# Shifted score powers and scaled V rows on GpSimd in a gated mix of attention and a Mish layer

## The chip, the cores and the metric

The kernel runs on one core of a Trainium2 chip. The metric is the device time of one execution in microseconds (us); lower is better. The engines are TensorE (PE in the profile, with PEld for its weight loads), VectorE (DVE), ScalarE (ACT), GpSimd (POOL) and SyncE (SP), which issues the DMAs.

## The reference

All inputs are bf16. `x` is 1 x 2048 x 640; there are 32 heads of width 20, and the hidden layer has 1536 columns.

```python
g = sigmoid((x * gate_w).sum(-1, keepdims=True))
q, k, v = split_heads(x @ wqkv)                      # 32 heads, Dh = 20
a = (softmax(q @ k.T * Dh ** -0.5) @ v).merge() @ wo
h = x @ w1 + b1
b = (h * tanh(softplus(h))) @ w2                     # Mish
out = g * a + (1 - g) * b
```

## The kernel before

Heads are taken four at a time (a quad, index `p`, eight of them), and queries 512 at a time (`qc`, four of them). A pair (p, qc) is a group `G`; there are 32. For each group and each block `j` of 128 keys, PE computes four score tiles, one per head: keys on partitions, 512 queries in one bank of PSUM (line 1127). Then comes exp, then the product with V (PV, line 1220), which sums over `j` in the last PSUM bank. V lies in `VA` with a column of ones, so that the sum of the exps comes out with the product; `normalise` divides by it.

The exps are made in two ways. Most go through ACT, two or three banks at an instruction (line 1177, into the ring `E`). The others, called sets in this text (one `j` of one group, all four heads), go through DVE. Line 437 turns a score tile into a power of two by writing a scaled and offset number as int16 and reading the bits as bf16, one instruction per head into a tile `T` of 128 x 2048. Two more tiles are made from `T` by adding a constant to each 16-bit word (line 495, `SHIFT` 43 and 86). The three tiles go into PV in turn, the shifted ones against copies of V scaled by 0.793 and 0.629 (`VD`, line 388). So the saw teeth of three approximations are averaged, and one set has three PVs of four matmuls in place of one. `VD` holds the last `ND` blocks of keys of a quad, and has three buffers for the eight quads. A shift may be placed only once its quad's `VD` is there.

PE also runs the dense products in pieces (chains: q and k, V, the hidden layer `h`, `w2`, `wo`), where four matmuls of 32 columns of the array stand side by side (`product`, line 531). ACT runs Mish twice, over half of the hidden layer each time (line 814), with a change of its function table before and after.

The whole order is made when the kernel is built, by a planner written into the kernel. It keeps a clock for PE, ACT and DVE, gives each instruction a fixed cost by its kind, and at each tick lets each free engine choose its next work by rules (`step_pe`, `step_act`, `step_dve`). The rules have some twenty parameters, changed as the groups advance by the table `PLAN`. The result is a fixed program: each engine runs its instructions in that order and waits on semaphores. PE does not pass over an instruction whose input is late.

In the tail of the kernel `b` (already multiplied by 1 - g and stored in DRAM, line 854) is loaded again a row block at a time (`load_b`, line 893) and added to the product with `wo` (line 933). `load_b` is called when a row's `wo` chain begins, for that row and the next one. All these DMAs stand in SP's queue in the order in which the planner calls them, with the stores of `o_dram` and the transposing loads of `od`.

```python
for eng in ("DVE", "ACT", "PE"):
    if free[eng] <= t:
        cost = steps[eng](t)
```

Of the kernel before, what the change touches and what calls it, by code (L numbers as in the profile page):

```python
# [11 lines left out]
ALU = mybir.AluOpType  # L12
F32 = mybir.dt.float32
BF16 = mybir.dt.bfloat16
I16 = mybir.dt.int16
F16 = mybir.dt.float16
PSUM = bass.MemoryType.PSUM
DEBUG = False


class Chain:
# [34 lines left out]
EXP_S2S = {3: 1331.0, 2: 904.0, 1: 520.0}  # L56
EXP_DUR = {3: 1460.0, 2: 1035.0, 1: 630.0}
DVE_TAIL = 100.0
INF = 1.0e18


@with_exitstack
def kernel(
# [33 lines left out]
    RATIO = (1.0, 0.79296875, 0.62890625)  # L97
    BETA = -210.4127
    LOG2E = 1.4426950408889634
    ND = 6  # L100
    NLAST = 3
    NSB = 2
    NFILL = 2
# [59 lines left out]
    rule.WAIT1 = 0.0  # L163
    rule.WAIT2 = 100000.0
    rule.WAITU = 100000.0
    PLAN = {
        0.0: {'AHEAD': 5000.0, 'BEHIND': 6000.0, 'D2': 0.5, 'DQ': 1, 'DQ3': 2, 'DQ4': 2, 'ETIGHT': 0, 'HEAT': 0.9, 'HROOM': 0.0, 'KEEP3': 3, 'LEAD': 6, 'LOW': 0.5, 'MARGIN': 60.0, 'MERGE': 0, 'NEAR': 9, 'NOPEN': 3, 'PVMAX': 4, 'Q3': 2, 'ROOM': 200.0, 'SWTH': 520.0, 'VF': 0, 'VMIN': 2, 'WAIT1': 2000.0, 'WAIT2': 6000.0, 'WAITU': 100000.0},
        1.0: {'DQ3': 1, 'HROOM': 100.0, 'LOW': 0.6, 'MARGIN': 0.0, 'SWTH': 600.0, 'WAIT2': 100000.0},
        2.0: {'DQ': 2, 'KEEP3': 1, 'MARGIN': 30.0},
        3.0: {'VMIN': 1},  # L170
        4.0: {'NOPEN': 4},
        5.0: {'AHEAD': 2000.0, 'DQ3': 0, 'MERGE': 1, 'Q3': 3},
        6.0: {'LOW': 0.44, 'MERGE': 0, 'NOPEN': 3, 'SWTH': 300.0, 'VF': 2, 'WAIT2': 30000.0},
        7.0: {'DQ4': 3, 'NEAR': 7},
        8.0: {'BEHIND': 2000.0, 'KEEP3': 2},
        9.0: {'D2': 1.0, 'HROOM': -200.0, 'NOPEN': 4, 'VF': 1, 'VMIN': 3},
        10.0: {'BEHIND': 6000.0, 'HEAT': 0.7, 'HROOM': 0.0, 'KEEP3': 3, 'LEAD': 5, 'LOW': 0.53, 'MARGIN': 100.0, 'PVMAX': 2, 'ROOM': 100.0, 'SWTH': 450.0, 'VMIN': 1},
        11.0: {'AHEAD': 3000.0, 'VF': 2},
        12.0: {'NEAR': 12},
        13.0: {'AHEAD': 5000.0, 'PVMAX': 3},  # L180
        14.0: {'AHEAD': 2000.0, 'BEHIND': 4000.0, 'DQ': 1},
        15.0: {'LOW': 0.47, 'NEAR': 9, 'WAITU': -200000.0},
        16.0: {'DQ': 2, 'DQ3': 3, 'PVMAX': 4, 'SWTH': 250.0, 'WAITU': 100000.0},
        17.0: {'BEHIND': 2000.0, 'HROOM': 100.0, 'SWTH': 600.0},
        18.0: {'KEEP3': 2, 'MARGIN': 0.0, 'PVMAX': 3},
        19.0: {'BEHIND': 3000.0, 'KEEP3': 3, 'MARGIN': 100.0, 'NEAR': 12},
        20.0: {'MARGIN': 60.0, 'Q3': 1, 'VF': 0},
        21.0: {'LOW': 0.38, 'NEAR': 9, 'WAITU': -200000.0},
        22.0: {'BEHIND': 2000.0, 'DQ': 1, 'DQ3': 0, 'LOW': 0.53, 'ROOM': 300.0},
        23.0: {'HEAT': 0.8, 'WAITU': 100000.0},  # L190
        24.0: {'BEHIND': 6000.0, 'DQ4': 0},
        25.0: {'DQ4': 1, 'PVMAX': 4, 'WAITU': -200000.0},
        26.0: {'NOPEN': 2, 'WAITU': 0.0},
        28.0: {'NOPEN': 4},
        29.0: {'HEAT': 0.7},
        30.0: {'HEAT': 0.8, 'NEAR': 99, 'PVMAX': 3, 'SWTH': 450.0},
    }

    x2d = A_x[0]
    out2d = out[0]  # L200
# [154 lines left out]
    dve_q = []  # L355
    act_q = deque()
    seq = [0]
    free = {"PE": 0.0, "ACT": 0.0, "DVE": 0.0}
    mode = [None]
    prog = [0.0]  # L360
    s_left = [64] * NG
    idle = {"PE": 0.0, "ACT": 0.0, "DVE": 0.0}

    def dve(t, ready, cost, fn, prio=1, done=None, can=None, born=INF):
        seq[0] += 1
        dve_q.append((prio, ready, seq[0], cost, fn, done, can, born))


    T_slots = [Slot(f"T{i}") for i in range(NHOLD)]
# [13 lines left out]
    def make_vd(p, t):  # L383
        VD[p] = work.tile([P, ND, NSH, 4 * (DH + 1)], BF16, tag=f"VD{p % NLAST}", name="VD")
        left = [NSH]

        def scale(i, t):
            nc.vector.tensor_scalar(
                out=VD[p][:, :, i, :],
                in0=VA[:, NS - ND : NS, 4 * p : 4 * p + 4, :].rearrange("p j h d -> p j (h d)"),  # L390
                scalar1=RATIO[i + 1], scalar2=None, op0=ALU.mult,
            )

        def done(t):
            left[0] -= 1
            if left[0] == 0:
                vd_ready[p] = t

        for i in range(NSH):
            dve(t, t, 200.0, (lambda t, i=i: scale(i, t)), prio=1, done=done)  # L400

    def backlog(t):

# [83 lines left out]
    def d_shifts(d, t):  # L487
        G, j = d["G"], d["j"]
        pv_items[G].append((t, j, (0, d["T"], d["slot"])))

        def shift(i, t):
            slot = t_slot(U_slots, t)
            slot.users = 4
            tile_ = work.tile([P, 4 * QC], BF16, tag=slot.tag, name="T")
            nc.vector.tensor_scalar(  # L495
                out=tile_[:, :].bitcast(I16), in0=d["T"][:, :].bitcast(I16),
                scalar1=float(SHIFT[i]), scalar2=None, op0=ALU.add,
            )
            d["T%d" % i] = (tile_, slot)
            d["slot"].users -= 1  # L500
            d["slot"].free_at = max(d["slot"].free_at, t + 700.0)

        def can(t):
            return (
                pv_G[0] >= G and vd_ready.get(groups[G][0], INF) <= t
                and t_slot(U_slots, t) is not None
            )

        for i in range(1, NSH + 1):
            dve(  # L510
                t, t, 600.0, (lambda t, i=i: shift(i, t)), prio=2, can=can,
                done=lambda t, i=i: pv_items[G].append((t, j, (i,) + d["T%d" % i])),
            )

# [306 lines left out]
    def b_chain(s, half, start, due):  # L821
# [19 lines left out]
        def evac():  # L841
            ps = box["ps"]

            def copy(t):
                if half == 0:
                    bt[s] = work.tile([P, D], BF16, tag=f"bt{s % 2}", name="bt")
                nc.vector.tensor_scalar(
                    out=bt[s][:, half * HALF : (half + 1) * HALF], in0=ps[:, :],
                    scalar1=g1_t[:, s : s + 1], scalar2=None, op0=ALU.mult,
                )  # L850

            def done(t):
                if half == 1:
                    nc.sync.dma_start(out=b_dram[s * P : (s + 1) * P, :], in_=bt[s][:, :])

            return [(420.0, copy)], done

# [27 lines left out]
    bl_slots = ["bl0", "bl1", "wkp"]  # L885
    bl_tag = {}

    def load_b(s):
        if s not in bl and s < NS and bl_slots and b_left[s // NU] == 0:
            bl_tag[s] = bl_slots.pop()  # L890
            pool_ = consts if bl_tag[s] == "wkp" else work
            bl[s] = pool_.tile([P, D], BF16, tag=bl_tag[s], name="bl")
            nc.sync.dma_start(out=bl[s][:, :], in_=b_dram[s * P : (s + 1) * P, :])
# [4 lines left out]
    def wo_chain(s, half, start, due):  # L898
# [6 lines left out]
        def piece(k, t):  # L905
            if k == 0:
                box["ps"] = bank_tile([P, HALF])
                begun.add(s)
                load_b(s)
                load_b(s + 1)  # L910
                assert s in bl
            r = min(P, rows - k * P)
            product(
                box["ps"][:, :],
                od[c][0:r, k, u * P : (u + 1) * P],
                wo_sb[0][0:r, k, cols],
                start=(k == 0),
                stop=(k == n - 1),
            )

        def evac():
# [16 lines left out]
            def done(t):  # L938
# [7 lines left out]

        return Chain(
            start, due, mm_pieces(n, piece, HALF / 2.4 + 3), evac,
            lambda t: o_ready.get(c, INF) <= t and (
                s in bl or (len(bl_slots) > 0 and b_left[c] == 0)  # L950
            ) and (s in begun if half else tail or ot_free.get(s % NOT, 0.0) <= t),
        )


# [466 lines left out]
    def enter(kind):  # L1421
        sw = switch(kind)
        mode[0], tiles[0] = kind, tiling(kind)
        return sw

    work_log = deque()
    heats = [0]

    def note(t, cost, weight):
        work_log.append((t, cost * weight))  # L1430
# [5 lines left out]

    def step_pe(t):
        units = s_ready(t)
        want = sum(ch.share(prog[0]) for ch in shares)
        d_take(t)  # L1440
        stuck_ = blocked(t)
        end = not peek(1)
# [74 lines left out]
        if units:  # L1517
# [20 lines left out]
                    break  # L1538
            enter("S")
            note(t, MM, 0.25 * len(used))  # L1540
            return cost
        until = max(slack, 0.0)
        if in_use(t) >= NOUT:
# [76 lines left out]
            done(t + cost + DVE_TAIL + SEM)  # L1620
        return cost

    steps = {"PE": step_pe, "ACT": step_act, "DVE": step_dve}
    t = 0.0
    stuck = 0
    vd_next = 0
    plan = sorted(PLAN)
    while pv_G[0] < NG or chains or chain[0] or dve_q or act_q:
# [3 lines left out]
        kq_loads(t)  # L1632
# [53 lines left out]
    for u, half, eng in ((2, 0, 0), (2, 1, 0), (3, 0, 0), (3, 1, 1)):  # L1686
# [4 lines left out]
            nc.vector.tensor_copy(out=dst, in_=src)  # L1691
        if half:
            nc.sync.dma_start(out=rows_[u], in_=ots_[u][:, :])
    if DEBUG:
        print("model end us", t / 1e3, "last exp", last_exp[0] / 1e3, {k: v / 1e3 for k, v in idle.items()}, "sets", sum(n_d), n_d, "heats", heats[0])

# [29 lines left out]
```

## Time and profile before

| | us |
|---|---|
| median of 3 runs | 731.72 |
| the runs | 731.72, 730.0, 732.04 |
| span of the profiled execution | 730.1 |
| ACT busy | 706.1 |
| PE busy | 713.1 |
| DVE busy | 683.7 |
| of it the shifts, 290 of 678 ns | 193.0 |
| POOL busy | 5.2 |

The span runs from the first to the last instruction of the profiled execution. The time of that one execution is not listed by itself; the lowest of the three runs is 0.1 us below its span and the median 1.6 us above, so sums made on the span are compared with the median by adding 1.6 us. "Busy" counts time in which an engine runs an instruction. The ends of matmuls are modelled, and PE also runs some filler products (line 1486), so 98% for PE does not mean that it has no room.

### The profile page before, as it was taken

The page shows a single profiled execution, that of the slowest core. Times are in us where ns is not written, and L with a number is a line of the kernel's source. Part 1 is how long each engine was busy: PE and PEld are TensorE (multiplying, and loading weights), DVE is VectorE, ACT ScalarE, POOL GpSimd, SP SyncE. Part 2 cuts the span into 40 slices and gives each one's busy share as a digit, 9 for nine tenths or more (in the row PEclk, how much of TensorE's full clock was granted, in tenths as well). Part 3 has the DMA queues.
Part 4 walks back from the last instruction along what each step waited for, and adds up shares of the span by engine and source line. Part 5 has one row for each costly group of instructions (what it writes and reads, how often), then busy time and mean ns, then how long its engine had stood idle before and what let it go on. Part 6 is the DMA issues. An engine that isn't in the chain of part 4 may idle for free.

```text
span 730.1 us, 24279 instructions
## 1 busy us (share of the span) xinstructions
PE 713.1 (98%) x10346; PEld 236.8 (32%) x10346; DVE 683.7 (94%) x1224; ACT 706.1 (97%) x729; POOL 5.2 (1%) x12
## 2 busy tenths in 40 slices
PE   8999999999999999999999999999999999999797
PEld 4433332233222333332332222222333333333233
DVE  4499999999999899999999999999999999999786
ACT  6899999999999999999999999999999999999886
POOL 2000000000000000000000000000000000000000
PEclk9999999999999999999999999999999999999989
DMA  9511221132402311101231224322102232213311
GB/s 248 174 26 32 50 44 43 41 63 54 92 20 49 50 35 16 16 27 27 47 91 34 47 49 97 63 43 46 40 13 64 38 50 50 50 24 71 79 56 56
DMA packets 125612, 40.46 MB, mean 55 GB/s; under 512 B 91136, under 2 KB 124944, under 8 KB 125504
## 3 DMA queue, kind: packets, MB, share of 16 engines
q1 hardware_dynamic: 123904, 38.38, 24.2%
q8 instruction: 81, 1.33, 0.8%
q10 hardware_dynamic: 1600, 0.53, 0.3%
q14 instruction: 27, 0.22, 0.1%
HBM read 23.61 MB, written 12.79 MB: 50 GB/s over the span
## 4 chain that ended last, share of the span: by engine, by line
PE 78%; ACT 12%; issue 4%; DMA 2%; DVE 2%; SPq 1%; DVEq 0%
PE Sp L1127 27%; PE Sp L531 26%; PE Sp L1220 24%; ACT E L1177 12%; DVE T L437 1%; DMA o_dram<-T 1%; DMA w_top<-in_A_wqkv_dram 1%; DMA q_dram<-st 1%; PE Sp L1486 0%; DMA bl<-b_dram 0%; PE Sp L1667 0%; PE Sp L1343 0%; DVE st L633 0%; DVE T L1241 0%; PE Sp L541 0%
## 5 line engine op out<-in xcount | busy, mean ns | idle before, releaser
L1177 ACT ACTIVATE E<-Sp 128x1024 bf16<-128x1024 f32 (+1 forms) x713 | 674.9, 1123 | 10.1 <-PE Sp L1127 9.7
L437 DVE TENSOR_SCALAR T<-Sp 128x512 int16<-128x512 f32 x580 | 378.9, 680 | 12.6 <-PE Sp L1127 10.8
L1127 PE MATMUL Sp<-qT,kT 32*128 32x512 bf16 x2048 | 288.4, 384 | 5.6 <-ACT E L1177 1.3
L495 DVE TENSOR_SCALAR T<-T 128x2048 int16<-128x2048 int16 x290 | 193.0, 678 | 0.1
L1127 PEld LDWEIGHTS <-kT 32*128 32x128 bf16 x2048 | 77.5, 91 | 265.0 <-issue 260.8
L1220 PE MATMUL Sp<-E,VA 128*21 128x512 bf16 x1468 | 140.3, 384 | 0.1
L1220 PE MATMUL Sp<-T,VD 128*21 128x512 bf16 x1160 | 110.2, 384 | 0.0
L531 PE MATMUL Sp<-w_sb,big 128*32 128x320 bf16 x1536 | 78.2, 301 | 0.0
L531 PE MATMUL Sp<-xT,w1t 128*32 128x512 bf16 x960 | 77.5, 384 | 0.1
L1220 PEld LDWEIGHTS <-VA 128*21 128x21 bf16 x2048 | 46.4, 90 | 66.7 <-issue 57.6
L1220 PE MATMUL Sp<-T,VA 128*21 128x512 bf16 x580 | 55.4, 384 | 0.0
L531 PE MATMUL Sp<-xT,ws 128*32 128x512 bf16 x720 | 53.8, 382 | 0.5 <-DVE st L633 0.5
L531 PEld LDWEIGHTS <-big 128*32 128x32 bf16 x1536 | 34.0, 95 | 27.5 <-issue 18.6
L1220 PEld LDWEIGHTS <-VD 128*21 128x21 bf16 x1160 | 28.7, 90 | 32.0 <-issue 26.0
L531 PE MATMUL Sp<-wo_sb,od 128*32 128x320 bf16 (+1 forms) x608 | 32.3, 307 | 4.2 <-DVE ot L933 4.2
L781 DVE TENSOR_SCALAR big<-Sp,b1f 128x512 bf16<-128x512 f32 x48 | 35.5, 739 | 0.8 <-PE Sp L531 0.7
L531 PE MATMUL Sp<-wv,xT 128*32 128x81 bf16 (+2 forms) x960 | 35.1, 258 | 0.2 <-DVE st L633 0.2
L531 PEld LDWEIGHTS <-w1t 128*32 128x32 bf16 x960 | 19.4, 94 | 29.5 <-issue 25.3
L633 DVE CAST st<-Sp 128x512 bf16<-128x512 f32 x36 | 24.4, 681 | 4.8 <-PE Sp L531 3.3
L531 PEld LDWEIGHTS <-xT 128*32 128x32 bf16 x960 | 18.5, 96 | 14.2 <-issue 11.6
L1241 DVE STREAM_TRANSPOSE T<-Sp 128x512 f32<-128x512 f32 x32 | 22.6, 707 | 0.4 <-PE Sp L1220 0.3
L716 DVE CAST VA<-Sp 128x80 bf16<-128x80 f32 (+2 forms) x48 | 16.0, 371 | 7.1 <-PE Sp L531 7.1
(72 smaller groups left out, 190.9 us busy)
## 6 DMA issues: line engine op xcount, KB each, us to landing
w1t<-in_B_w_dram SPq DMA_DIRECT2D x24, 320.0 KB
q_dram<-st SPq DMA_DIRECT2D x20, 128.0 KB
b_dram<-bt SPq DMA_DIRECT2D x16, 160.0 KB
bl<-b_dram SPq DMA_DIRECT2D x16, 160.0 KB
out_dram<-ot SPq DMA_DIRECT2D x16, 160.0 KB
qT<-q_dram SPq DMA_DIRECT2D x124, 20.0 KB
o_dram<-T SPq DMA_DIRECT2D x120, 20.0 KB
kT<-k_dram SPq DMA_DIRECT2D x28, 80.0 KB
```

The source lines that it names most:

```text
L437: nc.vector.tensor_scalar(out=dst.bitcast(I16), in0=src, scalar1=inv_sqrt_dh * LOG2E * 128.0, scalar2=127.0 * 128.0 + BETA, op0=ALU.mult, ...
L495: nc.vector.tensor_scalar(out=tile_[:, :].bitcast(I16), in0=d["T"][:, :].bitcast(I16), scalar1=float(SHIFT[i]), scalar2=None, op0=ALU.add,)
L531: nc.tensor.matmul(out_[k : k + 32], lhsT=lhsT[:, k : k + 32], rhs=rhs, tile_position=(0, k), **kw)
L633: nc.vector.tensor_copy(out=res["st"][:, :], in_=ps[:, :])
L716: nc.vector.tensor_copy(out=VA[:, sts[i], h0 : h0 + nh, 0:DH], in_=ps[:, i, 0:n].rearrange("p (h d) -> p h d", d=DH),)
L781: nc.vector.tensor_scalar(out=big[:, slot.tag, (ft % 2) * QC : (ft % 2 + 1) * QC], in0=ps[:, :], scalar1=b1f[:, ft : ft + 1], scalar2=None ...
L1127: nc.tensor.matmul(ps_cols, lhsT=kT[p][32 * t_ : 32 * t_ + 32, j * P : (j + 1) * P], rhs=qT[G][32 * t_ : 32 * t_ + 32, :], tile_position=( ...
L1177: nc.scalar.activation(E[:, x : x + n, :], ps, ACT.Exp, scale=inv_sqrt_dh,)
L1220: nc.tensor.matmul(acc[32 * t_ : 32 * t_ + DH + 1, :], lhsT=lhsT, rhs=rhs, start=(pv_done[G] == 0), stop=(pv_done[G] == pv_total[G] - 1), ...
L1241: nc.vector.transpose(out=st["T1"][:, :, :].rearrange("p b r -> p (b r)"), in_=acc[:, :])
```

## The change

- The shifts go from VectorE to GpSimd. `tensor_scalar` on int16 becomes `int64_add` on the same bytes seen as 64-bit integers, with the constant repeated in the four 16-bit fields of the addend. One instruction still does a whole tile.
- The scaling of V into `VD` goes to GpSimd too, with `op1=add` of 0.0 as second operation. `ND` becomes 7, so that an instruction scales 588 elements in place of 504.
- The planner gets a fourth engine, POOL, with a queue of its own (`gps`, `step_pool`) and costs of its own (`POOL_SHIFT`, `POOL_SCALE`, `POOL_TAIL`, in ns).
- The table `PLAN` is moved out of the function and has other values from start to end, so the order of the program is another one.
- `load_b` loads rows of b in sequence as soon as each is stored, a buffer is free and the o rows of its block are due soon by the plan, instead of when the row's `wo` chain begins.
- `kq_loads` and `load_b` are polled less often; the sum of the chains' shares is kept between steps; statistics are stored. These touch the order only.

```diff
+POOL_SHIFT = 1150.0
+POOL_SCALE = 900.0
+POOL_TAIL = 150.0
...
-    ND = 6
+    ND = 7
...
+    def gps(ready, cost, fn, done=None, can=None):
+        pool_q.append((ready, cost, fn, done, can))
...
         def scale(i, t):
-            nc.vector.tensor_scalar(
+            nc.gpsimd.tensor_scalar(
                 out=VD[p][:, :, i, :],
                 in0=VA[:, NS - ND : NS, 4 * p : 4 * p + 4, :].rearrange("p j h d -> p j (h d)"),
-                scalar1=RATIO[i + 1], scalar2=None, op0=ALU.mult,
+                scalar1=RATIO[i + 1], scalar2=0.0, op0=ALU.mult, op1=ALU.add,
             )
...
-            dve(t, t, 200.0, (lambda t, i=i: scale(i, t)), prio=1, done=done)
+            gps(t, POOL_SCALE, (lambda t, i=i: scale(i, t)), done=done)
...
-            nc.vector.tensor_scalar(
-                out=tile_[:, :].bitcast(I16), in0=d["T"][:, :].bitcast(I16),
-                scalar1=float(SHIFT[i]), scalar2=None, op0=ALU.add,
+            nc.gpsimd.int64_add(
+                tile_[:, :].bitcast(I64), d["T"][:, :].bitcast(I64), SHIFT[i] * 0x0001000100010001
             )
...
-            dve(
-                t, t, 600.0, (lambda t, i=i: shift(i, t)), prio=2, can=can,
+            gps(
+                t, POOL_SHIFT, (lambda t, i=i: shift(i, t)), can=can,
...
-    def load_b(s):
-        if s not in bl and s < NS and bl_slots and b_left[s // NU] == 0:
+    def load_b(t):
+        s = bl_next[0]
+        if s < NS and bl_slots and b_stored.get(s, INF) <= t and o_ready.get(s // NU, INF) <= t + 6000.0:
+            bl_next[0] += 1
+            bl_ready[s] = t + 3000.0
...
+    def step_pool(t):
+        for k, it in enumerate(pool_q):
+            if it[0] <= t and (it[4] is None or it[4](t)):
+                del pool_q[k]
+                _, cost, fn, done, _ = it
+                fn(t)
+                if done:
+                    done(t + cost + POOL_TAIL + SEM)
+                return cost
+        return None
...
-        for eng in ("DVE", "ACT", "PE"):
+        for eng in ("DVE", "ACT", "POOL", "PE"):
```

In the built program the sets go from 145 to 148, the shifts from 290 on DVE to 296 on POOL, and the exps on ACT from 671 of two banks and 42 of three to 641 and 58.

More of the change, by code (lines that the diff above doesn't have):

```diff
@@ L16 @@
 F16 = mybir.dt.float16
+I64 = mybir.dt.int64
 PSUM = bass.MemoryType.PSUM
 DEBUG = False
+STATS = {}
+PLAN = {
+    0.0: {'AHEAD': 1000.0, 'BEHIND': 6000.0, 'D2': 0.5, 'DQ': 2, 'DQ3': 2, 'DQ4': 2, 'ETIGHT': 0, 'HEAT': 0.9, 'HROOM': 0.0, 'KEEP3': 3, 'LEAD': 6, 'LOW': 0.5, 'MARGIN': 60.0, 'MERGE': 0, 'NEAR': 8, 'NOPEN': 3, 'PVMAX': 4, 'Q3': 2, 'ROOM': 200.0, 'SWTH': 520.0, 'VF': 0, 'VMIN': 2, 'WAIT1': 2000.0, 'WAIT2': 6000.0, 'WAITU': 0.0},
+    1.0: {'AHEAD': 5000.0, 'DQ3': 1, 'HROOM': 100.0, 'LOW': 0.65, 'MARGIN': 0.0, 'SWTH': 600.0, 'WAIT2': 100000.0, 'WAITU': 100000.0},
+    2.0: {'DQ4': 0, 'KEEP3': 1, 'MARGIN': 30.0, 'WAITU': 0.0},
+    3.0: {'DQ3': 0, 'DQ4': 2, 'LOW': 0.44, 'SWTH': 450.0, 'VMIN': 1, 'WAITU': 100000.0},
+    4.0: {'DQ3': 1, 'ETIGHT': 2, 'HROOM': 0.0, 'LOW': 0.5, 'NOPEN': 4, 'ROOM': 0.0, 'SWTH': 600.0, 'WAIT1': 0.0},
+    5.0: {'AHEAD': 8000.0, 'D2': 2.0, 'DQ3': 0, 'LOW': 0.6, 'Q3': 3, 'WAITU': 0.0},
+    6.0: {'LOW': 0.44, 'NOPEN': 3, 'ROOM': 200.0, 'VF': 2, 'WAIT2': 30000.0},
+    7.0: {'DQ4': 3, 'MARGIN': 0.0, 'SWTH': 300.0},
+    8.0: {'BEHIND': 2000.0, 'HEAT': 0.0, 'KEEP3': 3, 'MARGIN': 30.0, 'SWTH': 450.0},
+    9.0: {'DQ4': 2, 'HEAT': 0.8, 'HROOM': -200.0, 'LOW': 0.38, 'NOPEN': 4, 'Q3': 1, 'SWTH': 250.0, 'VF': 1, 'VMIN': 3, 'WAIT1': 2000.0},
+    10.0: {'BEHIND': 6000.0, 'DQ3': 1, 'DQ4': 3, 'HEAT': 0.7, 'LEAD': 4, 'LOW': 0.65, 'NEAR': 7, 'PVMAX': 2, 'ROOM': 100.0, 'VMIN': 1, 'WAIT1': 0.0, 'WAITU': -200000.0},
+    11.0: {'DQ3': 0, 'HROOM': 0.0, 'LEAD': 5, 'LOW': 0.53, 'NEAR': 12, 'ROOM': 0.0, 'SWTH': 450.0, 'VF': 2},
+    12.0: {'DQ4': 1, 'SWTH': 250.0, 'WAIT2': 100000.0, 'WAITU': 0.0},
+    13.0: {'HEAT': 0.9, 'LEAD': 7, 'LOW': 0.56, 'PVMAX': 4, 'WAIT1': 2000.0},
+    14.0: {'BEHIND': 4000.0, 'DQ': 3, 'DQ3': 1, 'LOW': 0.44, 'MARGIN': 60.0, 'ROOM': 100.0, 'WAIT1': 1000.0, 'WAIT2': 6000.0},
+    15.0: {'AHEAD': 1000.0, 'HEAT': 0.7, 'LEAD': 5, 'LOW': 0.56, 'MARGIN': 30.0, 'NEAR': 9, 'WAIT1': 2000.0},
+    16.0: {'DQ': 2, 'HROOM': 300.0, 'KEEP3': 2, 'LOW': 0.47, 'WAIT1': 4000.0},
+    17.0: {'BEHIND': 2000.0, 'DQ3': 0, 'DQ4': 3, 'WAIT1': 2000.0},
+    18.0: {'HROOM': 100.0, 'LOW': 0.38, 'MARGIN': 100.0, 'SWTH': 300.0, 'WAIT1': 4000.0, 'WAIT2': 30000.0},
+    19.0: {'BEHIND': 3000.0, 'LOW': 0.47, 'MARGIN': 30.0, 'NEAR': 12},
+    20.0: {'DQ': 3, 'MARGIN': -60.0, 'VF': 0},
+    21.0: {'DQ3': 2, 'DQ4': 1, 'KEEP3': 3, 'LOW': 0.38, 'MARGIN': 100.0, 'MERGE': 1, 'NEAR': 7, 'WAIT1': 2000.0},
+    22.0: {'BEHIND': 2000.0, 'DQ': 2, 'DQ4': 3, 'HROOM': 300.0, 'LOW': 0.53, 'MARGIN': 30.0, 'ROOM': 300.0, 'WAITU': 100000.0},
+    23.0: {'BEHIND': 3000.0, 'DQ3': 0, 'HEAT': 0.8, 'KEEP3': 2, 'LOW': 0.56, 'MARGIN': -60.0, 'NEAR': 9, 'NOPEN': 2, 'SWTH': 150.0, 'WAITU': 0.0},
+    24.0: {'DQ4': 0, 'HEAT': 0.0, 'KEEP3': 3, 'MERGE': 0, 'NOPEN': 5, 'SWTH': 600.0},
+    25.0: {'DQ4': 1, 'LOW': 0.53, 'MARGIN': 30.0, 'NOPEN': 4, 'ROOM': 100.0},
+    26.0: {'DQ': 3, 'LOW': 0.56, 'MERGE': 1, 'NOPEN': 3, 'SWTH': 150.0},
+    27.0: {'LOW': 0.53, 'NOPEN': 2},
+    28.0: {'AHEAD': 8000.0, 'BEHIND': 6000.0, 'MERGE': 0, 'NOPEN': 4, 'VF': 2, 'WAIT2': 100000.0, 'WAITU': 100000.0},
+    29.0: {'DQ': 1, 'DQ4': 3, 'WAIT1': 4000.0, 'WAIT2': 30000.0},
+    30.0: {'DQ4': 0, 'ETIGHT': 1, 'LEAD': 7, 'MARGIN': 0.0, 'WAITU': 0.0},
+    31.0: {'KEEP3': 9, 'LEAD': 5, 'PVMAX': 3, 'WAITU': -200000.0},
+}
@@ L165 @@
     rule.WAITU = 100000.0
[L166 to L197, printed above, removed]
     x2d = A_x[0]
@@ L357 @@
     seq = [0]
-    free = {"PE": 0.0, "ACT": 0.0, "DVE": 0.0}
+    free = {"PE": 0.0, "ACT": 0.0, "DVE": 0.0, "POOL": 0.0}
     mode = [None]
@@ L361 @@
     s_left = [64] * NG
-    idle = {"PE": 0.0, "ACT": 0.0, "DVE": 0.0}
+    idle = {"PE": 0.0, "ACT": 0.0, "DVE": 0.0, "POOL": 0.0}
+    pool_q = deque()
     def dve(t, ready, cost, fn, prio=1, done=None, can=None, born=INF):
@@ L500, in shift @@
             d["slot"].users -= 1
-            d["slot"].free_at = max(d["slot"].free_at, t + 700.0)
+            d["slot"].free_at = max(d["slot"].free_at, t + POOL_SHIFT + POOL_TAIL + SEM)
         def can(t):
@@ L854, in done @@
                     nc.sync.dma_start(out=b_dram[s * P : (s + 1) * P, :], in_=bt[s][:, :])
+                    b_stored[s] = t + 1000.0
             return [(420.0, copy)], done
@@ L886 @@
     bl_tag = {}
-    def load_b(s):
-        if s not in bl and s < NS and bl_slots and b_left[s // NU] == 0:
+    bl_next = [0]
+    bl_ready = {}
+    b_stored = {}
+    def load_b(t):
[3 more added lines that the diff above has]
+            bl_ready[s] = t + 3000.0
             bl_tag[s] = bl_slots.pop()
@@ L908, in piece @@
                 begun.add(s)
-                load_b(s)
-                load_b(s + 1)
                 assert s in bl
@@ L948, in wo_chain @@
             start, due, mm_pieces(n, piece, HALF / 2.4 + 3), evac,
-            lambda t: o_ready.get(c, INF) <= t and (
-                s in bl or (len(bl_slots) > 0 and b_left[c] == 0)
-            ) and (s in begun if half else tail or ot_free.get(s % NOT, 0.0) <= t),
+            lambda t: o_ready.get(c, INF) <= t and bl_ready.get(s, INF) <= t + 1000.0 and (s in begun if half else tail or ot_free.get(s % NOT, 0.0) <= t),
         )
@@ L1424, in enter @@
         return sw
+    shared = [None, 0.0]
+    visits = []
     work_log = deque()
@@ L1438, in step_pe @@
         units = s_ready(t)
-        want = sum(ch.share(prog[0]) for ch in shares)
+        if shared[0] != prog[0]:
+            shared[:] = prog[0], sum(ch.share(prog[0]) for ch in shares)
+        want = shared[1]
         d_take(t)
@@ L1540, in step_pe @@
             note(t, MM, 0.25 * len(used))
+            visits.append((len(units), len(used)))
             return cost
@@ L1621, in step_dve @@
         return cost
-    steps = {"PE": step_pe, "ACT": step_act, "DVE": step_dve}
+    def step_pool(t):
[8 more added lines that the diff above has]
+        return None
+    steps = {"PE": step_pe, "ACT": step_act, "DVE": step_dve, "POOL": step_pool}
     t = 0.0
@@ L1627 @@
     plan = sorted(PLAN)
-    while pv_G[0] < NG or chains or chain[0] or dve_q or act_q:
+    polled = 0.0
+    while pv_G[0] < NG or chains or chain[0] or dve_q or act_q or pool_q:
         while plan and prog[0] >= plan[0]:
@@ L1631 @@
         any_ = False
-        kq_loads(t)
+        if t >= polled:
+            polled = t + 100.0
+            kq_loads(t)
+            load_b(t)
         if vd_next < NQ and prog[0] > first[vd_next] - 1.0 and (
@@ L1693 @@
             nc.sync.dma_start(out=rows_[u], in_=ots_[u][:, :])
+    STATS.update(end=t / 1e3, exp=last_exp[0] / 1e3, idle=dict(idle), sets=sum(n_d), n_d=n_d, heats=heats[0], visits=visits)
     if DEBUG:
```

## The prediction

> **What bounds the kernel now.** I read the page's busy times first, then busy time by windows, then groups by shape, then the waits, and last POOL's own rows. The page has three engines close together, so it does not decide:
>
> ```profile
> PE 713.1 (98%) x10346; PEld 236.8 (32%) x10346; DVE 683.7 (94%) x1224; ACT 706.1 (97%) x729; POOL 5.2 (1%) x12
> ```
>
> The windows do. Columns: window, length, busy PE, PEld, DVE, ACT and POOL, granted clock, DMA share, GB/s.
>
> ```profile
> 100.00:150.00 50.00, 50.00 (x679) 14.60 (x675) 48.57 (x85) 50.00 (x52) 0.00 (x0) 1.00 0.23 47
> 450.00:500.00 50.00, 49.91 (x642) 13.72 (x638) 47.89 (x81) 50.00 (x54) 0.00 (x0) 1.00 0.26 57
> 690.00:700.00 10.00, 6.96 (x79) 2.00 (x78) 4.80 (x8) 4.01 (x5) 0.00 (x0) 0.66 0.40 118
> ```
>
> From 50 to about 688 us ACT is busy 49.9 to 50.0 of every 50 us. Its stream of exps, about 0.94 us each (23 in a row from 699.53 take 21.83), is the floor. DVE's load can shrink without ACT noticing. ACT loses time only at the start, in the tail, and in one hole at 690:
>
> ```profile
> DVE ot L933 <- DMA bl<-b_dram: 4.4, 1, 4.4
> PE Sp L531 <- DVE ot L933: 4.2, 1, 4.2
> ACT E L1177 <- PE Sp L1127: 9.7, 8, 4.3
> ```
>
> There a load of b's rows stands on SP behind transposes and a store, DVE waits for it, PE for DVE, ACT for PE. ACT loses 4.32, 0.87 and 0.80 us (timeline, 694 to 698), 6.0 in all for a wait of 4.43, since the clock falls to 0.66 and matmuls of 0.39 us take 0.65. So a PE stop of over 4 us costs its length and some 1.6 us more.
>
> **The change, part by part.** Groups that it touches, and POOL's rows, which are all there is to price POOL by:
>
> ```profile
> L1177 ACT ACTIVATE E<-Sp 128x1024 bf16<-128x1024 f32 x671 | 625.2, 1099 | 9.3 <-PE Sp L1127 8.9
> L1177 ACT ACTIVATE E<-Sp 128x1536 bf16<-128x1536 f32 x42 | 63.5, 1511 | 0.9 <-PE Sp L1127 0.9
> L495 DVE TENSOR_SCALAR T<-T 128x2048 int16<-128x2048 int16 x290 | 193.0, 678 | 0.1
> L388 DVE TENSOR_SCALAR VD<-VA 128x504 bf16<-128x504 bf16 x16 | 3.8, 282 | 0.0
> L1357 POOL MEMSET wo<- 128x640 bf16 x2 | 1.2, 632 | 4.8 <-PE Sp L1343 4.8
> masks.py:199 POOL TENSOR_SCALAR_AFFINE_SELECT ident<-ident 128x128 bf16<-128x128 bf16 x1 | 0.3, 294 | 0.1
> masks.py:199 POOLq MODIFY_POOL_CONFIG  x2: 12/12/12, 0.9 to 1.0; - x2
> ```
>
> *DVE loses* 193.0 + 3.8 us and falls to about 68% busy. Gain: 0, because ACT did not wait for it.
>
> *ACT.* The built program has 641 two-bank and 58 three-bank exps (before 671 and 42): the new rules send 148 sets to DVE instead of 145. By busy time each (625.2 / 671 = 0.932, 63.5 / 42 = 1.512), 30 x 0.932 = 28.0 us go and 16 x 1.512 = 24.2 come: -3.8. By pitch (0.94, and 0.94 + 0.41 for a third bank) it is -6.6. I take -5. PE is even: six more PV slots, nine fewer fillers, two fewer score visits.
>
> *b's rows* are loaded up to three ahead, so the hole should close: -6.0, or 0 if SP is late again. The 16 issues of 0.43 us stay; they now pass out_dram stores and q loads on SP.
>
> *The shifts* become 296 POOL instructions over 1024 words. By the memset (0.99 ns an element) one takes 1.01 us, by the select (2.3) 2.35. I take 1.15, the cost the new planner works with, near the first. V's scale over 588 elements is 0.58 to 1.35; I take 0.9. POOL's sum is 296 x 1.15 + 16 x 0.9 = 355 us, so it has room. Each PV that reads a shifted T now waits for POOL, and behind it on PE stand the scores of the next exps.
>
> *What the diff does not show.* The order on POOL has 21 instructions more, without operands: each asks for another instruction library, number 1 ahead of shifts and 0 ahead of V's scale. After the first, they come as ten round trips, away from the shifts and back. The trace has such a request once, for library 0 at the start, the MODIFY_POOL_CONFIG row: 12 ns, and the select follows 0.06 us later. But nothing had displaced that library. The lower bound of a real switch is therefore 0.06 us. For the rest the nearest rows are a read out of DRAM and the table load by which ACT changes its function:
>
> ```profile
> 2.12 4.51 DMA w_top<-in_A_wqkv_dram
> L814 ACT ACT_TABLE_LOAD x2 | 2.6, 1283 | 0.0
> ```
>
> Read and take over: 4.51 + 1.28 = R = 5.8 us a switch. Upper bound, both configuration steps with a read each, 9.0. I take 5.8, since code that was overwritten must be fetched, as the DMA row is and the resident request is not. The Trainium skill, "GPSIMD Engine Reference", section 2.1, says that the first call to a freshly loaded GpSimd kernel pays about 6 us (5.95) for loading its code. The row of 12 ns is not of that size, and no run so far shows a changed library. By that figure the sum would be 3 us higher.
>
> *What a round trip costs.* I count in exps along PE's order: a, the exps whose scores stand ahead of the last power before the trip; b, those ahead of the first PV that needs a shift made after it. POOL is free about 3.7 us after a (0.4 scores, 0.68 power and some queue, two shifts). Slack = (b - a) x 0.94 - 3.7 - scales x 0.9 - 1.15. The stop on PE is 2R = 11.6 less the slack:
> 89 to 104, two scales: slack 7.4; 154 to 162, two: 0.9; 324 to 331, one: 0.8; 328 to 342, one: 7.4; 410 to 421, two: 3.7; 432 to 441, one: 2.7; 437 to 445, one: 1.8; 459 to 469, two: 2.7. Together 27.4 of slack, so the eight stops are 92.8 - 27.4 = 65.4 us. Two more trips (243 to 249, 247 to 250) lie at the first Mish, which occupies ACT for 1.28 + 10.44 + 1.28 = 13.0 us without scores. From its start PE stops 11.7, then has 216 matmuls to the second trip's PV (about 14 us at the trace's 15 to 17 a us), by when that trip is over: 25.7 less 13.0 and two buffered exps (1.9), about 11. The first switch, ahead of the first shift, is late by about 1. The cooler clock adds 8 x 1.6 = 13.
>
> Sum on the span: 730.1 - 5 - 6 + 65.4 + 11 + 1 + 13 = 809.5. The span is 1.6 below the median of 731.72, so 811 us.
>
> **Rivals.**
> *Switches cost next to nothing.* The 12 ns row speaks for it; against it, that request changed nothing. Then only ACT's saving and the closed hole count: 730.1 - 11 + 1.6 = 721 (715 to 727 by the bounds above). This ends on the other side. It decides from R of about 1.7 us down: there the stops are 2.5, 2.6, 0.7, 1.6 and 0.7, with 2.5 at the Mish: 10.6 us, about what is gained. At 4 us the result is about 773. By the figure of the Trainium skill's "GPSIMD Engine Reference" (section 2.1) this rival is out.
> *The shift itself is slow.* At the select's rate, 2.35 us, a set's pair takes 4.7 us of the 4.9 at which sets come (730 / 148), and the second shift lands 2.4 us behind plan where gaps of three or four exps leave nothing. POOL is then the bound: 296 x 2.35 + 21 x 5.8 + 14 + 30 at the start = 862 us. For it, the select; against it, the memsets, and the planner's 1.15.
> *The switch is longer*, 9.0 us by both steps: eight stops of together 8 x 18 - 27.4 = 116.6, 24 at the Mish: 730.1 - 11 + 116.6 + 24 + 2 + 13 + 1.6 = 876.
>
> **How the numbers follow.** Switches of about 4 to 8 us with shifts near plan: 0.66, 773 to 855, most likely 811. Short ones of 2.2 to 4 us: 0.08, 733 to 773. Shift at the select's rate, or switches near 9 us: 0.08, 855 to 880. Switches next to free: 0.16, near 721. Even, within 0.3% (about 2 us, what a measurement of this kernel can tell from no change): 0.02. The range 738 to 880 leaves out the free switch, the even case and the edge of the short one, 2 in 10. Faster 0.16, same 0.02, slower 0.82.
>
> **What would show it.** In the changed profile: POOL gaps of 5 to 6 us ahead of each V scale and each shift after it; PE's PV (L1235) waiting for POOL's T some ten times, the longest near 11 us, 70 to 80 in all; PEclk with dips; ACT idle by about 100 us more; DVE near 494 us busy; a shift near 1.15 us; no wait for bl. I am wrong if the gaps are under 2 us, if PE never waits for POOL more than 2 us, or if the waits are spread evenly over all shifts, which would be the slow shift.

## The result, and the profile after

| | before | after |
|---|---|---|
| median, us | 731.71 (730.0 to 732.04) | 823.89 (822.64 to 826.26) |
| span of the profiled execution, us | 730.1 | 822.7 |
| ratio, 95% interval | | 1.127, 1.125 to 1.129 |

The change makes the kernel 92 us slower; the forecast was 811 us, in a range of 738 to 880. Medians and ratios, here and below, are of fast runs alone; one run of all was slow, at 868.43 us, the fourth of e11. The page of the changed kernel, busy times and the granted clock by slices:

```profile
PE 727.0 (88%) x10334; PEld 235.5 (29%) x10334; DVE 551.7 (67%) x927; ACT 703.3 (85%) x715; POOL 320.2 (39%) x324
...
PEclk9999998997999889999789997769899999999999
```

No engine is full any more, POOL least of all. The work that ACT has to do fell from 706.1 to 703.3 us; what grew is the time in which it has none. The waits, with the sum in us, the number of times and the longest, say who withholds it:

```profile
ACT E L1192 <- PE Sp L1142: 98.4, 40, 11.8
PE Sp L1235 <- POOL T L507: 77.5, 11, 11.3
PE Sp L1334 <- POOL ident masks.py:199: 5.9, 1, 5.9
POOL ident masks.py:199 <- issue: 8.6, 1, 8.6
```

ACT waits for scores, PE for a shifted tile, and only eleven times for 296 shifts. The mean alone, 7 us a time, says that this is not a matter of how fast a shift is. The groups of POOL's two operations, with the number, the busy time, the mean in ns, and the idle time ahead of them:

```profile
L507 POOL INT64_ADD T<-T x296 | 304.2, 1041 | 374.8 <-DVE T L449 124.5
L400 POOL TENSOR_SCALAR VD<-VA 128x588 bf16<-128x588 bf16 x16 | 10.8, 675 | 102.3 <-issue 37.6
```

A shift takes 1.04 us, a V scale 0.68. Sixteen scales, 11 us of work, have 102 us of idle time ahead of them. Of these, 29 us stand ahead of the first pair, which waits for VectorE at the start of the kernel. The other 73 us lie in ten places, 6.8 to 7.8 us each, and the shifts behind these ten places have another 60 us ahead of them, 5.7 to 6.4 us each. The profile puts five of the ten gaps ahead of scales down to "issue" and the others to VectorE or PE, but their lengths are alike. One round trip, in POOL's timeline and in PE's (start, length, and in brackets the idle time before it):

```profile
184.35 1.41 POOL L400 TENSOR_SCALAR VD<-VA 128x588 bf16<-128x588 bf16 x2 [7.84 <-issue]
191.64 2.05 POOL L507 INT64_ADD T<-T  x2 [5.88 <-issue]
```

```profile
192.72 0.61 PE L1235 MATMUL Sp<-T,VD 128*21 128x512 bf16 x4 [11.34 <-POOL T L507]
```

"Issue" means that the engine waited for nothing that the profile shows. The scales stand 7.84 us behind the shifts ahead of them, the next shifts 5.88 us behind the scales, and no instruction fills either stretch: the rows of the request for a library, two for each request, are 1 to 11 ns long ahead of shifts (and at most 13 ahead of scales):

```profile
L507 POOLq MODIFY_POOL_CONFIG  x22: 1/1/11, 47.6 to 572.8; - x22
```

PE meets the first late tile after a wait of 11.34 us, and its first matmuls take 0.61 us instead of 0.39. The trace stops here without a verdict on one point: it shows that the gaps lie around the scales, not that the library is what fills them. That is the first question for the experiments.

### The profile page after: what moved, and what is told of

It is laid out like the page before. It is cut to its first block, busy times and chain, and to the rows that moved or that the text cites. A ratio compares the mean times of both kernels' runs of the same rounds, so it can differ in the third digit from the quotient of the medians.

```text
span 822.7 us, 24573 instructions
## 1 busy us (share of the span) xinstructions
PE 727.0 (88%) x10334; PEld 235.5 (29%) x10334; DVE 551.7 (67%) x927; ACT 703.3 (85%) x715; POOL 320.2 (39%) x324
## 5 line engine op out<-in xcount | busy, mean ns | idle before, releaser
L449 DVE TENSOR_SCALAR T<-Sp 128x512 int16<-128x512 f32 (+1 forms) x589 | 397.7, 690 | 203.4 <-PE Sp L1142 192.5
L507 POOL INT64_ADD T<-T x296 | 304.2, 1041 | 374.8 <-DVE T L449 124.5
L1235 PE MATMUL Sp<-T,VD 128*21 128x512 bf16 x1184 | 116.8, 395 | 77.5 <-POOL T L507 77.5
L1142 PEld LDWEIGHTS <-kT 32*128 32x128 bf16 x2048 | 74.6, 91 | 270.1 <-issue 265.7
L542 PE MATMUL Sp<-xT,w1t 128*32 128x512 bf16 x960 | 81.2, 395 | 0.0
L542 PE MATMUL Sp<-w_sb,big 128*32 128x320 bf16 x1536 | 80.9, 306 | 0.0
L542 PE MATMUL Sp<-xT,ws 128*32 128x512 bf16 x720 | 58.4, 406 | 0.0
L400 POOL TENSOR_SCALAR VD<-VA 128x588 bf16<-128x588 bf16 x16 | 10.8, 675 | 102.3 <-issue 37.6
```

Of the source, the lines that this page charges most:

```text
L400: nc.gpsimd.tensor_scalar(out=VD[p][:, :, i, :], in0=VA[:, NS - ND : NS, 4 * p : 4 * p + 4, :].rearrange("p j h d -> p j (h d)"), scalar1= ...
L449: nc.vector.tensor_scalar(out=dst.bitcast(I16), in0=src, scalar1=inv_sqrt_dh * LOG2E * 128.0, scalar2=127.0 * 128.0 + BETA, op0=ALU.mult, ...
L507: nc.gpsimd.int64_add(tile_[:, :].bitcast(I64), d["T"][:, :].bitcast(I64), SHIFT[i] * 0x0001000100010001)
L542: nc.tensor.matmul(out_[k : k + 32], lhsT=lhsT[:, k : k + 32], rhs=rhs, tile_position=(0, k), **kw)
L1142: nc.tensor.matmul(ps_cols, lhsT=kT[p][32 * t_ : 32 * t_ + 32, j * P : (j + 1) * P], rhs=qT[G][32 * t_ : 32 * t_ + 32, :], tile_position=( ...
L1235: nc.tensor.matmul(acc[32 * t_ : 32 * t_ + DH + 1, :], lhsT=lhsT, rhs=rhs, start=(pv_done[G] == 0), stop=(pv_done[G] == pv_total[G] - 1), ...
```

## The experiments

The theory: every change between a shift and a V scale makes POOL load another library, some 6 us each way; PE stops for the two switches less the slack that the plan left between the trip and the first PV that needs it; the rest of the change gains some 10 us. Rivals: the shift's own rate; contention of the moved work with other engines; a fixed price for each trip. Each ratio is against the kernel before, run beside it on the same chip.

**e1: the scales back on VectorE, the order made anew.**

```diff
-            nc.gpsimd.tensor_scalar(
+            nc.vector.tensor_scalar(
...
-                scalar1=RATIO[i + 1], scalar2=0.0, op0=ALU.mult, op1=ALU.add,
+                scalar1=RATIO[i + 1], scalar2=None, op0=ALU.mult,
...
-            gps(t, POOL_SCALE, (lambda t, i=i: scale(i, t)), done=done)
+            dve(t, t, 200.0, (lambda t, i=i: scale(i, t)), prio=1, done=done)
```

> The scaling of V goes back to VectorE, the shifts stay on GpSimd, so that the ten round trips between libraries go; one switch stays at the start and one ahead of the first shift. Theory (the switches make the loss): PE's waits for POOL fall from 77.5 us to under 5, the slow matmuls after each stop go with them, and the time is 727 us: the 721 of free switches and some 6 us for the select that still waits at the start. Rival (the shifts on POOL are late by themselves, through their length or by sharing with VectorE): PE still waits for POOL by tens of us, over 760 us.

Measured: 743.76 us, ratio 1.015 (1.011 to 1.018). Eighty us come back by moving 11 us of work, and PE waits for no shifted tile any more. But it is 17 us above what was expected. POOL's select at the start, which makes the identity for PE's first transposes, is late here too:

```profile
9.75 0.28 POOL masks.py:199 TENSOR_SCALAR_AFFINE_SELECT ident<-ident 128x128 bf16<-128x128 bf16 x1 [8.77 <-issue]
```

PE waits 6.1 us for it. The expectation had put 6 us for this, so it explains little of the 17. Most of the rest is a hole of 12.86 us in ACT's stream that ends at 212 us. e2 has it too.

**e2: as e1, with the shifts' library named once at the top, so that nothing is ever switched.**

```diff
+    from concourse import library_config
+    nc.gpsimd.load_library(library_config.all_libraries[1])
     zero_w = consts.tile([P, 32], BF16, tag="zero_w")
```

> As the kernel with the scaling on VectorE, and library 1, which also holds the select of the start, is named at the top, so that nothing is switched. Theory: the select starts near 1 us instead of 9.6, PE's wait of 5.9 us for it goes, 721 us. Rival (the late start has another cause, such as a slower first load): equal to the kernel that only moves the scaling.

Measured: 737.59 us, ratio 1.007 (1.005 to 1.009); span 733.6, 8.4 us less than e1's. The gap at the start is gone, so the first request, too, has a price. The expected 721 us was missed. PE waits for nothing of POOL's; ACT's timeline, and then PE's, shows where the time is:

```profile
203.37 1.94 ACT L1194 ACTIVATE E<-Sp 128x1024 bf16<-128x1024 f32 x2 [11.86 <-PE Sp L1144]
```

```profile
200.51 1.92 PE L544 MATMUL Sp<-xT,w1t 128*32 128x512 bf16 x20 [2.93 <-DMA w1t<-in_B_w_dram]
```

Before ACT's row PE does dense chains for 12 us without a score, and for 2.93 us of these it waits for a weight tile that such a chain needs. With the scales on DVE at 200 ns the planner's clock runs differently, it puts 150 sets on DVE instead of 148, and the same table of rules gives an order with a hole. So e1 and e2 changed two things, and the next run keeps the order.

**e8: the order of the changed kernel, instruction for instruction; VectorE makes the scales, and the shifts' library is named at the top.** The planner still counts the scales as POOL's, so that it decides all else alike.

```diff
+    from concourse import library_config
+    nc.gpsimd.load_library(library_config.all_libraries[1])
...
-            nc.gpsimd.tensor_scalar(
+            nc.vector.tensor_scalar(
...
-                scalar1=RATIO[i + 1], scalar2=0.0, op0=ALU.mult, op1=ALU.add,
+                scalar1=RATIO[i + 1], scalar2=None, op0=ALU.mult,
```

> The order of the changed kernel kept as it is: the planner still counts V's scales as POOL's, but VectorE runs them, and library 1 is named at the top, so that no switch is left. Theory (the switches are the whole loss, and the 737.6 of the replanned kernel is the hole of 11.9 us that its other order has near 191 us): 714 to 724 us, PE waits for POOL under 5 us. Rival (shifts on POOL or the new rules cost some 15 us by themselves): 735 to 740 us.

Measured: 723.24 us, ratio 0.990 (0.988 to 0.991), faster than both kernels. The page:

```profile
span 721.1 us, 24531 instructions
...
PE 707.5 (98%) x10334; PEld 233.8 (32%) x10334; DVE 554.6 (77%) x943; ACT 699.8 (97%) x715; POOL 309.5 (43%) x308
```

POOL makes the same 296 shifts, and no wait of PE for POOL is left. So the shifts on POOL, their rate and whatever they contend for are not what costs; the sixteen scales on POOL and the requests around them cost 101.6 us of span.

**e3: as e2, with the table of rules of before.**

```diff
-    0.0: {'AHEAD': 1000.0, 'BEHIND': 6000.0, ...
+    0.0: {'AHEAD': 5000.0, 'BEHIND': 6000.0, ...
```

> Shifts on POOL in one library, scales on VectorE, b's rows ahead, but the table of rules of the kernel before. Theory (a table of rules fits the one order that it was picked for): an order with holes in ACT's stream, 725 to 745 us, and no waits for POOL over 3 us. Rival (rules matter little): within 4 us of the kernel in one library with the new rules, 737.6.

Measured: 741.63 us, ratio 1.016 (1.014 to 1.018), with holes in ACT's stream of 4.54 and 2.87 us and 11.96 us idle at its end, where e8 has 3.12. That lies where the theory put it, but the median is only 4.04 us above e2's, at the edge of what the rival allows. Against the kernel before, run beside each, it is 0.9% above e2, some 7 us. One other table does not show that a table fits only the order that it was picked for. Neither e2 nor e3 tells what an order made for their model would give.

**e4: the kernel before, with the new `load_b` alone.** The condition is that of the diff; `load_b` is called at every step of the planner.

```diff
-    def load_b(s):
-        if s not in bl and s < NS and bl_slots and b_left[s // NU] == 0:
+    def load_b(t):
+        s = bl_next[0]
+        if s < NS and bl_slots and b_stored.get(s, INF) <= t and o_ready.get(s // NU, INF) <= t + 6000.0:
...
```

> The kernel before with the new loading of b's rows alone. By the prediction's step: the wait for b near 690 us goes and with it the slow matmuls, 6 us less than before. Rival: the row is late for the same transposes and stores on SP, no change.

Measured: 725.5 us, ratio 0.994 (0.992 to 0.995), 4.7 us gained. The hole at 690 us is closed; the window of 20 us around it has ACT (fourth busy time) full:

```profile
680.00:700.00 20.00, 19.90 (x314) 7.27 (x311) 18.88 (x35) 20.00 (x21) 0.00 (x0) 1.00 0.39 92
```

**e5: the kernel before, with eight round trips on a scratch tile for which nobody waits.**

```diff
...
     def make_vd(p, t):
+        nc.gpsimd.int64_add(scr2[:, :].bitcast(mybir.dt.int64), scr[:, :].bitcast(mybir.dt.int64), 0)
+        nc.gpsimd.tensor_scalar(
+            out=scr2[:, :], in0=scr[:, :], scalar1=1.0, scalar2=0.0, op0=ALU.mult, op1=ALU.add
+        )
```

> The kernel before, order kept, with eight round trips on POOL beside it: at each quad one add on a small scratch tile under library 1 and one scale of it under library 0, which nobody waits for. Theory: POOL's gaps are 6 us toward library 1 and 7 to 8 toward library 0, and the time is that of before within 1 us, since a switch costs only what waits for POOL. Rival (a switch slows the chip's other engines, through instruction fetch or DMA): 5 us or more above before.

Measured: 730.14 us, ratio 1.000 (0.998 to 1.001). The gaps are there without anything else that the change does:

```profile
39.30 0.29 POOL L389 TENSOR_SCALAR scr<-scr 128x128 bf16<-128x128 bf16 x1 [6.82 <-issue]
45.47 0.23 POOL L388 INT64_ADD scr<-scr  x1 [5.88 <-issue]
```

The eight gaps ahead of an INT64_ADD are 7.2 (the first) and then 5.8 to 6.4 us, those ahead of a TENSOR_SCALAR 6.8 to 8.0. This is the price of a switch by itself, and alone it costs the kernel nothing, so a switch does not measurably slow the other engines either. It costs only where PE waits for what is behind it.

**e6: the changed kernel, with the standard library asked for behind the last shift.**

```diff
+    from concourse import library_config
+    nc.gpsimd.load_library(library_config.standard)
     tx, ty = allb[:, 0:3, :], allb[:, 3:6, :]
```

> The changed kernel, with library 0 asked for again behind the last shift. Theory (an execution starts with the library that the one before it left): the select at the start no longer waits, 5.9 us less, 818 us. Rival (the first request always costs, and 1.07 us in the kernel before was something else): no change, 824 us.

Measured: 819.32 us, ratio 1.117 (1.114 to 1.121); span 816.6, 6.1 us less. The select starts at once:

```profile
1.28 0.29 POOL masks.py:199 TENSOR_SCALAR_AFFINE_SELECT ident<-ident 128x128 bf16<-128x128 bf16 x1 [0.29 <-POOL ident masks.py:197]
```

So the changed kernel ends with the shifts' library loaded, and the next execution begins by paying for the other one. A request at the end, where nobody waits, takes this out. e2 differs from e1, and e6 from the changed kernel, by a request for a library alone, and in both the gap of over 8 us at the start goes. So it is the library that fills it, which the trace of the changed kernel alone did not show.

**e7: both scales of a quad as one item of POOL's queue: seven trips, order made anew.**

```diff
-        for i in range(NSH):
-            gps(t, POOL_SCALE, (lambda t, i=i: scale(i, t)), done=done)
+        def both_scales(t):
+            for i in range(NSH):
+                scale(i, t)
+        left[0] = 1
+        gps(t, NSH * POOL_SCALE, both_scales, done=done)
```

> The changed kernel with a quad's two scales placed one behind the other, so that there are seven round trips in place of ten (the planner orders anew). Theory: each of the three second trips falls out of the sum with its stop, 3 + 4 + 10 us by the prediction's working and some 5 us of slower clock: 798 to 808 us. Rival (the loss does not go by trips): within 5 us of 824.

Measured: 814.73 us, ratio 1.112 (1.109 to 1.116), between theory and rival. PE's waits for POOL fall from 77.5 us in 11 to this:

```profile
PE Sp L1239 <- POOL T L511: 67.0, 9, 12.5
```

Three trips of ten fewer save 10.5 us of 77.5: the ten trips stopped PE for 7.7 us each, the seven stop it for 9.4. The order was made anew, so the slack of each trip changed; it was not worked out for this order. The run does not separate "fixed price" from "price less slack"; the next two do.

**e9 and e10: e8 with one trip given back.** In e9 it is that of quad 1, to which the prediction gave 7.4 us of slack; in e10 that of quad 2, with 0.9.

```diff
-            nc.vector.tensor_scalar(
+            (nc.gpsimd if p == 1 else nc.vector).tensor_scalar(
```

> The order of e8 (723.2 us) with VectorE doing all V scales but the two of one quad, which GpSimd does between the shifts, so that one round trip between its libraries comes back. In the order's plan this trip had 7.4 us of slack. Theory (a trip costs TensorE two switches, some 13 us with the lengths of after, less the plan's slack): a stop of about 3.5 to 4 us at that set (after: 3.48), and about 1 us of slower clock behind it: 727 to 728 us, ratio about 1.006. Rival (a trip costs a fixed price, 101.6 us over ten trips, whatever its slack): 733 us, the same as e10.

> As e9, but the one trip is that of the next quad, which had 0.9 us of slack in the plan. Theory: a stop of about 11 us at that set (after: 11.34), and about 2 us of slower clock and exps behind it: about 736 us, ratio about 1.018, 8 to 9 us above e9. Rival (fixed price): 733 us, no difference from e9.

Measured: e9 729.25 us, ratio 0.995 (0.992 to 0.997); e10 737.86 us, ratio 1.007 (1.004 to 1.009). The kernel before ran some 2 us higher beside these two than beside e8, so the ratios are compared: against e8's 0.990, e9 costs 0.5% or 3.5 us, e10 1.7% or 12.2 us, and between them lie 8.6 us. PE's timeline of e9, then of e10:

```profile
121.41 0.61 PE L1237 MATMUL Sp<-T,VD 128*21 128x512 bf16 x4 [3.90 <-POOL T L509]
```

```profile
182.80 0.61 PE L1237 MATMUL Sp<-T,VD 128*21 128x512 bf16 x4 [11.26 <-POOL T L509]
```

Two switches around two scales stop PE for 3.9 us in one place and 11.3 in the other. A fixed price per trip would have given 733 us twice. The difference in slack, 6.5 us by the plan, is 7.4 us on PE; 0.4 of that is a longer pair of switches (13.6 us for 13.2).

**e11: e8 with every shift issued twice.**

```diff
-            nc.gpsimd.int64_add(
-                tile_[:, :].bitcast(I64), d["T"][:, :].bitcast(I64), SHIFT[i] * 0x0001000100010001
-            )
+            for _ in range(2):
+                nc.gpsimd.int64_add(
+                    tile_[:, :].bitcast(I64), d["T"][:, :].bitcast(I64), SHIFT[i] * 0x0001000100010001
+                )
```

> The order of e8 with every shift issued twice, so that a set of two shifts takes 4.2 us instead of 2.1; no trips. It tries the prediction's slow-shift rival, which put 2.3 us for a shift at 862 us. Busy time of GpSimd becomes 300 + 309 = about 620 us, below the span. Theory of the rival: the sets of shifts now end later than the order wants them, TensorE waits for GpSimd at many sets by 1 to 2 us each, and the time is above 800 us. Counter-theory: the plan's slack of three to four exps between a set and its use takes up 2.1 us, so that the time stays below 745 us.

Measured: 857.03 us, ratio 1.169 (1.164 to 1.174). This is the prediction's slow shift, 2.08 us in place of 1.04, and its sign is the one that the prediction named, waits spread over many sets:

```profile
PE 746.4 (88%) x10334; PEld 240.7 (28%) x10334; DVE 562.6 (66%) x943; ACT 717.6 (84%) x715; POOL 617.0 (72%) x604
```

```profile
ACT E L1195 <- PE Sp L1145: 116.8, 139, 4.8
PE Sp L1238 <- POOL T L510: 93.0, 117, 1.8
```

POOL is busy 72% of the span, so it is not the bound by its sum: the second shift of a set lands some 2 us later, and 117 times there was not enough slack for that. So the counter-theory is out: the plan of the changed kernel has little room beyond what its shifts take.

## Why the prediction was right, step by step

**DVE's loss gains nothing: right.** In e8 DVE is 77% busy and the kernel 1% faster than before, which ACT's work and b's rows cover (below). The forecast "near 494 us" was wrong: 551.7. The groups of shifts and scales, 197 us, were subtracted whole from the engine's busy time, which fell by 132. Before, DVE's groups add up to 749 us while the engine was busy for 683.7: neighbours overlap, and the engine's sum counts that stretch once. After, the groups add up to 576 for 551.7, so 41 us of the 65 that are missing are overlap that went with the shifts; most of the rest is the powers' group, 397.7 us for 378.9. The share of 67% in the changed kernel matches the forecast's 68% only because the span grew.

**ACT's work: right in busy time.** 30 two-bank exps fewer and 16 three-bank ones more: 705.6 us in e4, 699.8 in e8, so 5.8 for the 5 of the sum. In the span e8 gains 2.5 us on e4 (723.6 and 721.1): ACT is busy 25.94 us of the 30 between 20 and 50 us in e8 and 28.56 before, so the new order starts worse.

**b's rows: right.** 4.7 us for 6 (e4). The hole is not the same in every execution: DVE's wait for b is 4.4 us in the trace of before and 2.9 in that of e5, whose order is the same.

**The base without switches.** The sum has 730.1 - 11 = 719.1; e8's span is 721.1. The rival of the free switch, 721 us in the median, is what e8 measures: 723.24. Its mechanism is sound, its condition false.

**The price of a switch: right in size, one size for two.** R was put at 5.8 us from a DMA read and a table load. The trace has 5.8 to 6.4 us toward the shifts' library and 6.8 to 8.0 toward the standard one (e5), 13.3 a round trip against 11.6. The 1.7 us missing in each trip hardly showed, because other terms erred the other way (next paragraph). That R came out of rows of other mechanisms, and the lower bound was 100 times less, makes this a good guess more than a reading. The price of a shift, 1.15 us, was the new planner's, and the reading that was to support it does not: the memset's 0.99 ns was multiplied by 1024 words, while the instruction adds 512 words of 64 bits, for which that rate gives 0.51 us and the trace 1.04. The Trainium skill, "GPSIMD Engine Reference", section 2.1, puts the first call to a freshly loaded GpSimd kernel at approximately 6 us, "with no visible profile instruction". The trace agrees for the way to the shifts' library: a gap of 5.88 us in the trip shown, and request rows of 1 to 11 ns. The way back is longer, 7.84 us in that trip.

**Stop = two switches less slack: right as a rule; its numbers met by two errors that cancel.** PE's waits for POOL in order of time; the two at the Mish, 243 and 247, were put together as ACT's loss:

| trip (exps a to b) | stop predicted, us | PE waited, us | ACT idle there, us |
|---|---|---|---|
| first shift | 1 | 0.55 | 0.56 |
| 89 to 104 | 4.2 | 3.48 | 6.0 |
| 154 to 162 | 10.7 | 11.34 | 12.4 |
| 243, 247 (Mish) | 11 for ACT | 11.16 + 2.33 | 15.8 |
| 324 to 331 | 10.8 | 10.48 | 12.1 |
| 328 to 342 | 4.2 | 3.57 | 5.3 |
| 410 to 421 | 7.9 | 7.30 | 9.1 |
| 432 to 441 | 8.9 | 8.84 | 10.6 |
| 437 to 445 | 9.8 | 9.82 | 12.3 |
| 459 to 469 | 8.9 | 8.63 | 9.6 |

The eight that were worked out by slack add up to 65.4 predicted and 63.5 measured. That is closer than the terms deserve. With the measured lengths (13.3 us for two switches, 0.68 a scale, 1.04 a shift) the same formula gives 75.4 us. In every one of the eight trips the order left POOL 1.0 to 2.0 us more than the formula's (b - a) x 0.94 - 3.7, together 11.5 us. The two shifts in the 3.7, at 1.04 for 1.15, are 0.2 us of it each time; where the rest lies was not tried. So the size of a single stop is known from this formula to 2 us or so, not better. e9 and e10 show that the rule is cause and not only arithmetic: one trip alone, in the same order, has its own stop again (3.90 and 11.26).

**The clock after a stop: right.** 8 x 1.6 = 13 was charged. ACT's idle time at the eight is 77.4, 13.9 more than PE's wait. ACT's timeline behind the stop of 8.84 us shows how:

```profile
530.93 1.02 ACT L1192 ACTIVATE E<-Sp 128x1024 bf16<-128x1024 f32 x1 [9.15 <-PE Sp L1142]
532.86 1.02 ACT L1192 ACTIVATE E<-Sp 128x1024 bf16<-128x1024 f32 x1 [0.91 <-PE Sp L1142]
534.37 1.02 ACT L1192 ACTIVATE E<-Sp 128x1024 bf16<-128x1024 f32 x1 [0.49 <-PE Sp L1142]
```

PE's scores take 0.61 us until 535 and 0.39 after, so exps come half a microsecond late each for some 5 us. The Trainium skill, "TensorE: Matmul & The Clock Gate", Part 1, has the clock fall after a window of about 3.4 us without work. The stops of 3.48 and 3.57 us agree, they were followed by scores of 0.61, and that of 0.55 was not. But the stop of 2.33 us that ended at 305.37 was, too. The windows around it (columns as in the prediction) are these:

```profile
302.00:306.00 4.00, 1.67 (x42) 0.97 (x34) 1.65 (x3) 0.00 (x0) 1.71 (x2) 1.00 0.02 5
306.00:310.00 4.00, 4.00 (x53) 1.12 (x45) 1.38 (x2) 2.05 (x2) 2.12 (x3) 0.57 0.10 25
```

PE was busy for 1.67 us of the 4 from 302 to 306, and from 306 to 310 the granted clock was 0.57. So a stop shorter than that window was followed by the lower clock here, and the measurement decides; what the shortest such stop is was not tried.

**The Mish: too low.** The sum had 14 us of matmuls between the two stops, by when the second trip would be over, and two buffered exps for ACT. In the trace the dense products behind the first stop end 9.7 us after it, one exp was buffered, and what follows is the scores of a set for DVE, the second stop of 2.33 us, and the low clock again. ACT is idle for 8.05 and for 6.88 us around a single exp, in all 15.8 us instead of 11.

**The first request: missed.** The prediction read the request at the start as free, since nothing had displaced the library. In the changed kernel the execution before it has: 6.2 us on ACT (first exp at 17.10 us for 10.88 in e8), taken out in e6 (6.1) and shown from the other side by e1 and e2 (8.4).

The forecast's 811 against 823.9 us is thus: the start 6.2; the Mish 4.8; the base 2.0; longer ACT instructions 3.5 (703.3 busy for e8's 699.8: an exp that follows idle time stands at 1.02 us, eight in a row at 7.44); less 1.0 for the eight stops with their clock, 0.4 for the first shift, and 2.7 for a small gap of e8 at 46 us that the changed kernel does not have. That is 12.4, and the spans differ by 822.7 - 809.5 = 13.2.

**The rivals.** Free switch: out, by the gaps of e5. Switch of 9 us: out, the longest to the standard library are 8.0. Slow shift: did not happen (1.04 us), but its price was too low. 862 us had been worked out as POOL's sum, with 21 switches and 30 us at the start in it; e11 reaches 857.03 with no switch at all and POOL 72% busy, through PE's 117 waits for a late tile. That the two figures are close is chance.

## What to carry to other kernels

Where an order is fixed, price a delay by the slack of the instruction that needs its result and not by the engine's busy share: the same two switches cost nothing in e5, 3.5 us in e9 and 12.2 in e10. Suspect idle time that returns with nearly the same length wherever an operation of another kind follows, and test it as a cost of that change, whatever the profile names as its end: here 11 us of V scales on GpSimd brought 101.6 us with them, and e8, which leaves them on VectorE and the shifts on GpSimd, is the fastest of all (723.24 us, 0.990 of before). When one part of such a change is to be tried alone, keep the order of the instructions: with the order made anew the kernel stands 12 us (e2) and 19 us (e3) above e8 by the ratios, though all three have the scales on VectorE and no switch.

## What was not expected of the hardware

- A change of GpSimd's library is not the same both ways: 5.8 to 6.4 us to the one with the 64-bit add (7.2 the first time), 6.8 to 8.0 back to the one with TENSOR_SCALAR (e5). The rows of the request itself are 1 to 13 ns long in the trace of the changed kernel.
- The library stays loaded from one execution to the next: a kernel that ends with another one than it begins with pays at its start (a gap of 8.6 us, and none in e6).
- GpSimd adds a constant to 512 64-bit words in each of 128 partitions in 1.04 us (1.03 at the least); VectorE took 0.68 us for the same bytes as int16. GpSimd's TENSOR_SCALAR over 588 bf16 took 0.68.
- What makes the way back to the standard library longer, and the first way out of e5 7.2 us long, was not tried.
